# Two attention and GLU layers on one core: half of the values' products of the second layer as three f16 rounds, the GLU remainder on GpSimd

## The chip, the cores and the metric

The kernel runs on one core of one Trainium2 chip. The metric is device time in microseconds (us) of one execution; lower is better. The kernel before takes 2244.29 us, the median of 3 runs (2242.11 to 2247.71). The engines are written as the profile writes them: PE is TensorE (PEld its weight loads), DVE is VectorE, ACT is ScalarE, POOL is GpSimd, SP is SyncE, which issues most DMAs.

## The reference

x is 1 x 2048 x 448 in f32. There are 16 heads of 28, with one key head and one value head that all query heads share. F is 1792.

```python
def _A_ref(x, wq, wk, wv, wo):
    q = (x @ wq).reshape(B, S, H, Dh).transpose(0, 2, 1, 3)
    k, v = x @ wk, x @ wv
    p = softmax(einsum("bhqd,bkd->bhqk", q, k) * Dh ** -0.5)
    o = einsum("bhqk,bkd->bhqd", p, v)
    return o.transpose(0, 2, 1, 3).reshape(B, S, H * Dh) @ wo

def _B_ref(x, w_gate, w_up, w_down):
    return (sigmoid(x @ w_gate) * (x @ w_up)) @ w_down

x = x + _A_ref(layernorm(x), ...)      # layer 1
x = x + _B_ref(layernorm(x), ...)
x = x + _A_ref(layernorm(x), ...)      # layer 2, same weights
x = x + _B_ref(layernorm(x), ...)
```

## The kernel before

**Tiling.** The 2048 positions are cut into 16 *units* of 128 queries. In each layer a unit `u` runs through 16 *steps* `kt`, one for each 128 keys; so a layer has 256 steps. The 16 heads lie in 4 groups `g` of 4 heads, so that one group's queries make a moving operand of 4 x 128 = 512 columns. Two consecutive steps, an even and an odd one, are called a *pair* below.

**One step.** `scores` multiplies 128 keys with the queries of a group into the PSUM tile `s` (128 x 512, f16 operands), and ACT takes the exponent of `s` into the f32 SBUF tile `P`; four times in a step. `pv` multiplies `P` with the values `VV` (f32, 32 columns: 28 of the values and a column of ones for the softmax's sum). Its four matmuls, one for each group, occupy four different strips of 32 columns of the array (`tile_position=(0, 32 * g)`) and run at the same time; they add into one PSUM tile `pv` over the 16 steps. Each f32 matmul stands in the trace as two records. `Maxima.step` computes scores of a later unit against all keys (tiles `mx`, four matmuls at a time in four strips of 32 rows) and DVE reduces each `mx` tile to a row maximum; the maxima enter the scores of that later unit through an extra row. So in layer 2 DVE makes four reductions of 128 x 512 in each step up to unit 14.

**Order.** Every engine runs its instructions in the order in which the program writes them. The order is set by strings in `PATHS`: S is a `scores`, P a `pv` of the oldest waiting step, M a `Maxima.step`, X a tick of the side work, F a slice of filler. In layer 2, units 4 to 13 use D0 (even units) and D1 (odd units), units 14 and 15 E0 and E1. The first string of each serves even steps, the second odd steps. Both P of a pair stand in the even step and take the two steps of the pair before it. Filler is all other TensorE work, metered by `Filler.slice`: the GLU's gate and up products (`gp`, `up`), the down products (`dn`) and the output projection (`wo`). Work of other engines that follows a filler product is put off by `defer(fn, lag)` and written out at a later slice (`flush`).

**GLU.** Per block of 256 positions, 7 times: ACT makes `th` = tanh of the gate product, DVE makes (th + 1) x up in `th` (L756), ACT rounds it to f16 as `h[:, 0]` (L759), and DVE makes the remainder `h[:, 1]` (L760). `dn` multiplies both with the f16 halves of `w_down`.

**Side work of a unit** comes once in 16 steps, through ticks: the softmax sums go out and come back by DMA (`sums`, `rc`, `lb`), GpSimd multiplies (`lb`, L671), ACT and DVE split into two f16 parts (`oT`, L677 and L678), then the `wo` products, then on DVE the residual (L693) and the layer norm's statistics (L292, L293), six small GpSimd instructions for the reciprocal root (`rs`, L308 to L313), on DVE `xn` and `hl` (L331, L323), on GpSimd the remainder of `hl` (L324, L325).

**PSUM.** All tiles but `pv` share one ring of 7 banks (tag "f"). A matmul that opens a new tile waits until the tile that had the bank seven tiles earlier has been read by DVE or ACT.

Of the kernel before, what the change touches and what calls it, by code (L numbers as in the profile page):

```python
# [19 lines left out]
def interleaved_layers_kernel(ctx: ExitStack, tc: tile.TileContext, x, wq, wk, wv, wo, wg, wu, wd, out, layers=2):  # L20
# [147 lines left out]
    def prep_b():  # L168
# [75 lines left out]
        nc.vector.tensor_scalar(gsc, pwb[:, 1:2], 2.0 ** -26, None, op0=OP.mult)  # L244
# [40 lines left out]
    def ln_stats(*xts, fast=False):  # L285

        n = len(xts)
        mv = wk1.tile([128, 4, 2], F32, name="mv", bufs=4)
        r = wk1.tile([128, 4, 4], F32, name="rs", bufs=4)
        for i, xt in enumerate(xts):  # L290
            st = wk1.tile([128, 6], F32, name="st", bufs=3)
            nc.vector.bn_stats(st, xt)  # L292
            nc.vector.bn_aggr(mv[:, i], st)  # L293
        return (rstd_v if fast else rstd)(mv, r, n)
# [11 lines left out]
    def rstd(mv, r, n, bias=False):  # L306
# [5 lines left out]
        nc.gpsimd.tensor_scalar(z, z, -1024.0, 3072.0, op0=OP.mult, op1=OP.add)  # L312
# [52 lines left out]
    KK, VV, QH = {}, {}, {}  # L365

    def layer_tiles(l):
# [215 lines left out]
    def scores(l, u, kt, g, P):  # L583
# [4 lines left out]
        p = wk1.tile([128, 512], F32, tag="P", name="P", bufs=14)  # L588
        nc.scalar.activation(p, s, AF.Exp, scale=esc)  # L589
        P.append(p)  # L590

    def pv(l, u, kt, P):
# [3 lines left out]
        for g in range(4):  # L596
            nc.tensor.matmul(v[32 * g:32 * g + 32], VV[l][:, kt], P[g], start=kt == 0, stop=kt == KT - 1,  # L597
                             tile_position=(0, 32 * g))
# [25 lines left out]
    class Block:  # L624
# [8 lines left out]
        def tile(self, u):  # L633
# [53 lines left out]
            def wo_products():  # L687
# [4 lines left out]
                def f():  # L692
                    nc.vector.scalar_tensor_tensor(self.x1[:, t], p, osc, v["xr"], op0=OP.mult, op1=OP.add)  # L693
                    v["ls"] = ln_stats(self.x1[:, t])[0]
# [39 lines left out]
        def bulk(self):  # L734
# [3 lines left out]
            def glu(f):  # L738
# [15 lines left out]
                def ev():  # L754
# [3 lines left out]
                    def parts():  # L758
                        nc.scalar.activation(h[:, 0], t, AF.Copy, scale=2.0 ** -17)  # L759
                        defer(lambda: nc.vector.scalar_tensor_tensor(h[:, 1], t, 2.0 ** -17, h[:, 0], op0=OP.mult,  # L760
                                                                     op1=OP.subtract), 3)
# [272 lines left out]
    for b in range(1, NB):  # L1034
# [15 lines left out]
        "D0": ("FXFFSSSSPPM", "FSFSFXSFFMS"),  # L1050
        "D1": ("SFFXSFSSPPM", "SFSFFFXSFSFM"),
# [130 lines left out]
```

## Time and profile before

| | |
|---|---|
| median of 3 runs | 2244.29 us (2242.11 to 2247.71) |
| profiled execution, span from first to last instruction | 2242.6 us |
| mean granted TensorE clock | 0.996 |
| PE busy, share of the span | 98% |
| DVE busy | 73% |
| ACT busy | 69% |
| POOL busy | 15% |
| units 4 to 15 of layer 2 | about 1410 to 2157 us |
| one unit there | 62 to 64 us; unit 15: 52 us |

In rows of groups the two numbers after the bar are the busy time in us and the mean of one instruction in ns, then the engine's idle time before them with what ended it. In rows of a timeline the first number is the start in us, the second the duration; a merged row lasts from the first start to the last end, and brackets hold the idle time before it. Consecutive matmuls overlap in the trace, so the time a matmul costs is read from the start of the next one.

### The profile page before, as it was taken

What the parts mean: (1) busy time and instruction counts of PE and PEld (TensorE: products, weight loads), DVE (VectorE), ACT (ScalarE), POOL (GpSimd) and SP (SyncE); (2) the same over time, 40 slices, a digit from 0 to 9 for tenths busy, and PEclk for the clock granted to TensorE, in tenths of its full rate; (3) what the DMA queues carried; (4) which work ended last, traced back from release to release, by engine and by line L of the source; (5) the groups of instructions that cost most, each with busy time, mean ns of one, the idle gap of its engine ahead of it and who ended that gap; (6) DMA issues with size and microseconds to landing.
All of it is one profiled execution on the core that took longest, in us unless ns stands there. A gap on an engine that the chain in (4) does not pass through costs nothing.

```text
span 2242.6 us, 41405 instructions
## 1 busy us (share of the span) xinstructions
PE 2197.5 (98%) x15922; PEld 1032.1 (46%) x15922; DVE 1633.7 (73%) x2902; ACT 1556.5 (69%) x2603; POOL 328.6 (15%) x567
## 2 busy tenths in 40 slices
PE   7899999999999999999999999999999999999999
PEld 3322344444444444454564334445454545445457
DVE  7888887778778777777796557777777777777222
ACT  5698887777667677676514997777676767777741
POOL 4123764001110100101011010000000000000010
PEclk9999999999999999999999999999999999999999
DMA  5232662324323132422441123232231313132333
GB/s 174 70 98 87 209 211 83 105 62 118 98 67 102 58 109 61 127 78 69 135 136 40 31 56 113 52 107 80 86 101 58 107 50 104 56 107 78 97 105 118
DMA packets 203622, 213.28 MB, mean 95 GB/s; under 512 B 135376, under 2 KB 164240, under 8 KB 203424
## 3 DMA queue, kind: packets, MB, share of 16 engines
q1 hardware_dynamic: 198880, 195.88, 29.6%
q0 software_dynamic: 4544, 14.77, 1.7%
q8 instruction: 124, 2.03, 0.4%
q14 instruction: 74, 0.61, 0.1%
HBM read 175.37 MB, written 23.59 MB: 89 GB/s over the span
## 4 chain that ended last, share of the span: by engine, by line
PE 86%; DVE 4%; DMA 2%; ACT 2%; issue 1%; SPq 1%; POOL 0%; ACTq 0%; POOLq 0%; DVEq 0%
PE pv L597 20%; PE s L586 20%; PE dn L786 11%; PE gp L354 11%; PE up L354 11%; PE mx L551 7%; PE wo L697 3%; DVE mp L556 3%; PE qp L354 2%; ACT P L589 1%; DMA rc<-sums 1%; DMA sums<-rc 0%; DMA rgu<-in_B_w_gate_dram 0%; DMA lb<-sums 0%; PE hot L918 0%
## 5 line engine op out<-in xcount | busy, mean ns | idle before, releaser
L589 ACT ACTIVATE P<-s,esc 128x512 f32<-128x512 f32 x2048 | 1295.7, 692 | 455.8 <-PE s L586 444.6
L556 DVE TENSOR_REDUCE mp<-mx 128x1 f32<-128x512 f32 x2048 | 1269.6, 683 | 387.1 <-PE mx L551 382.7
L586 PE MATMUL s<-QS,KK 96*128 96x512 f16 x2048 | 687.0, 382 | 13.3 <-DVE mp L556 9.0
L354 PEld LDWEIGHTS <-wgu 128*128 128x128 f16 x4928 | 470.6, 97 | 174.6 <-issue 30.1
L597 PE MATMUL pv<-P,VV 128*32 128x512 f32 x4096 | 510.3, 602 | 0.0
L354 PE MATMUL gp<-XT,wgu 128*128 128x256 f16 x2464 | 350.3, 272 | 0.8 <-DVE mp L556 0.8
L354 PE MATMUL up<-XT,wgu 128*128 128x256 f16 x2464 | 347.7, 272 | 0.0
L786 PE MATMUL dn<-WD,h 128*128 128x448 f16 x1344 | 299.9, 352 | 0.0
L586 PEld LDWEIGHTS <-KK 96*128 96x128 f16 x2048 | 190.7, 97 | 232.6 <-issue 142.2
L597 PEld LDWEIGHTS pv<-P,VV 128*32 128x32 f32 x4096 | 98.7, 108 | 240.1 <-issue 238.9
L551 PE MATMUL mx<-KK,QH 32*128 32x512 f16 x1792 | 186.8, 384 | 5.3 <-DVE mp L556 1.9
L786 PEld LDWEIGHTS <-h 128*128 128x128 f16 x1344 | 127.1, 97 | 127.6 <-issue 11.2
L551 PEld LDWEIGHTS <-QH 32*128 32x128 f16 x1792 | 46.5, 91 | 247.8 <-issue 245.4
L671 POOL TENSOR_TENSOR lb<-pvs,lb 128x512 f32<-128x512 f32 x32 | 41.2, 1287 | 622.3 <-DMA lb<-sums 548.7
L759 ACT ACTIVATE h<-th 128x512 f16<-128x512 f32 x112 | 70.4, 628 | 67.4 <-DVE th L756 67.3
L308 POOL TENSOR_SCALAR rs<-mv 128x1 f32<-128x1 f32 (+1 forms) x50 | 12.2, 244 | 678.0 <-DVE mv L293 676.0
L354 PE MATMUL qp<-XT,WQ 128*128 128x512 f16 x352 | 109.5, 389 | 1.0 <-DVE mp L556 0.7
L756 DVE SCALAR_TENSOR_TENSOR th<-th,up 128x512 f32<-128x512 f32 x112 | 76.2, 680 | 42.2 <-PE up L354 36.7
L748 ACT ACTIVATE th<-gp,gsc 128x512 f32<-128x512 f32 x112 | 76.8, 686 | 32.3 <-PE gp L354 32.2
L760 DVE SCALAR_TENSOR_TENSOR h<-th,h 128x512 f16<-128x512 f32 x112 | 77.0, 688 | 29.6 <-ACT h L759 29.6
L697 PE MATMUL wo<-WO,oT 128*128 128x448 f16 x384 | 88.8, 352 | 0.9 <-ACT oT L677 0.5
L354 PEld LDWEIGHTS <-WQ 128*128 128x128 f16 x352 | 33.6, 99 | 49.7 <-issue 23.1
(158 smaller groups left out, 908.2 us busy)
## 6 DMA issues: line engine op xcount, KB each, us to landing
wgu<-wgu_d SPq DMA_DIRECT2D x224, 512.0 KB
QS<-qd SPq DMA_DIRECT2D x384, 32.0 KB
lb<-sums SPq DMA_DIRECT2D x128, 64.0 KB
xr<-in_A_x_dram SPq DMA_DIRECT2D x32, 224.0 KB
qd<-qst POOLq DMA_DIRECT2D x28, 256.0 KB, 2.6
wgu_d<-sgu POOLq DMA_DIRECT2D x14, 512.0 KB, 4.0
x2d<-x SPq DMA_DIRECT2D x16, 224.0 KB
xr<-x2d SPq DMA_DIRECT2D x16, 224.0 KB
```

Source lines behind the costliest of these rows:

```text
L354: nc.tensor.matmul(ps, a, b, start=n == 0, stop=n == 10)
L551: nc.tensor.matmul(ps[h][:, i * w:(i + 1) * w], qh[32 * h:32 * h + 32, g], KK[l][32 * h:32 * h + 32, 1, ka:kz], start=True, stop=True, til ...
L556: nc.vector.tensor_reduce(o, ps[h].rearrange("p (g k) -> p g k", g=n), axis=AX.X, op=OP.max)
L586: nc.tensor.matmul(s, KK[l][0:96, 0, kt * 128:(kt + 1) * 128], QS[l, u][:, g].rearrange("p h n -> p (h n)"), start=True, stop=True)
L589: nc.scalar.activation(p, s, AF.Exp, scale=esc)
L597: nc.tensor.matmul(v[32 * g:32 * g + 32], VV[l][:, kt], P[g], start=kt == 0, stop=kt == KT - 1, tile_position=(0, 32 * g))
L697: nc.tensor.matmul(p, v["oT"][:, a, h * 128:(h + 1) * 128], WO[:, c, h], start=n == 0, stop=n == 11)
L748: defer(lambda: nc.scalar.activation(th, gp.rearrange("p j n -> p (j n)"), AF.Tanh, scale=gsc))
L756: nc.vector.scalar_tensor_tensor(t, th, 1.0, up.rearrange("p j n -> p (j n)"), op0=OP.add, op1=OP.mult)
L759: nc.scalar.activation(h[:, 0], t, AF.Copy, scale=2.0 ** -17)
L760: defer(lambda: nc.vector.scalar_tensor_tensor(h[:, 1], t, 2.0 ** -17, h[:, 0], op0=OP.mult, op1=OP.subtract), 3)
L786: nc.tensor.matmul(p, hs[f // 2][:, a, o:o + 128], WD[:, f, c], start=n == 0, stop=n == 3 * FC - 1)
```

## The change

In layer 2, for even steps of units 4 to 15 (12 units x 8 steps = 96 steps), `P` and the values are each split into two f16 parts, high and remainder, and `pv` makes three rounds of four f16 matmuls (high x high, high of P x remainder of V, remainder of P x high of V) where it made four f32 matmuls. The high part of P is cast by DVE for groups 0 and 1 and by ACT for groups 2 and 3; the remainder is a GpSimd subtraction for all four. The parts lie in tiles `PH` of the pool `big`, three pairs of parts to a tile. The values' parts `VH` are made by GpSimd when layer 2's values are made. The ring of `P` shrinks from 14 to 13 tiles. The GLU remainder `h[:, 1]` moves from DVE to GpSimd in both layers, and is now a plain subtraction: the power-of-two factor 2^-17 has moved into the layer norm's factor and the scales. The strings D0 and D1 are written anew.

```diff
+            if l in VH:
+                nc.gpsimd.tensor_copy(VH[l][:, kt, 0], VV[l][:, kt])
+                nc.gpsimd.tensor_tensor(VH[l][:, kt, 1], VV[l][:, kt], VH[l][:, kt, 0], op=OP.subtract)
...
-        p = wk1.tile([128, 512], F32, tag="P", name="P", bufs=14)
+        p = wk1.tile([128, 512], F32, tag="P", name="P", bufs=13)
         nc.scalar.activation(p, s, AF.Exp, scale=esc)
-        P.append(p)
+        if not halved(l, u, kt):
+            P.append(p)
+            return
+        if not hold or hold[1] == 3:
+            hold[:] = [big.tile([128, 7, 512], F16, tag="big", name="PH"), 0]
+        t, n = hold
+        hold[1] += 1
+        hi, lo = t[:, 2 * n], t[:, 2 * n + 1]
+        P.append((hi, lo))
+        how = HI[g]
+
+        def part():
+            if how == "a":
+                nc.scalar.copy(hi, p)
+            else:
+                (nc.vector if how == "d" else nc.gpsimd).tensor_copy(hi, p)
+            nc.gpsimd.tensor_tensor(lo, p, hi, op=OP.subtract)
+        defer(part, HLAG)
+
+    hold = []
+    HI, HLAG = "ddaa", 2
+
+    def halved(l, u, k):
+        return l and u > 3 and k % 2 == 0
...
-        for g in range(4):
-            nc.tensor.matmul(v[32 * g:32 * g + 32], VV[l][:, kt], P[g], start=kt == 0, stop=kt == KT - 1,
-                             tile_position=(0, 32 * g))
+        if halved(l, u, kt):
+            flush(True)
+            for n, (a, c) in enumerate(((0, 0), (1, 0), (0, 1))):
+                for g in range(4):
+                    nc.tensor.matmul(v[32 * g:32 * g + 32], VH[l][:, kt, a], P[g][c],
+                                     start=kt == 0 and n == 0, stop=kt == KT - 1 and n == 2,
+                                     tile_position=(0, 32 * g))
+        else:
+            for g in range(4):
+                nc.tensor.matmul(v[32 * g:32 * g + 32], VV[l][:, kt], P[g], start=kt == 0, stop=kt == KT - 1,
+                                 tile_position=(0, 32 * g))
...
                     def parts():
-                        nc.scalar.activation(h[:, 0], t, AF.Copy, scale=2.0 ** -17)
-                        defer(lambda: nc.vector.scalar_tensor_tensor(h[:, 1], t, 2.0 ** -17, h[:, 0], op0=OP.mult,
-                                                                     op1=OP.subtract), 3)
+                        nc.scalar.copy(h[:, 0], t)
+                        nc.gpsimd.tensor_tensor(h[:, 1], t, h[:, 0], op=OP.subtract)
                     defer(parts, 3)
...
-        "D0": ("FXFFSSSSPPM", "FSFSFXSFFMS"),
-        "D1": ("SFFXSFSSPPM", "SFSFFFXSFSFM"),
+        "D0": ("FSFSXFSSPPM", "FSFFSXSFFMS"),
+        "D1": ("FSFSXFSSPPM", "FSFSFXSFSFM"),
```

Three places in the order of the instructions follow. The first is TensorE's order at the two P of a pair in layer 2. Before, with the last `scores` ahead of it and the first maxima behind it (`VV` values, `QH` queries for the maxima):

```order
L586 LDWEIGHTS KK
L586 MATMUL s<-QS,KK 128x512
L597 MATMUL pv<-P,VV 32x512 x8
L551 LDWEIGHTS QH
L551 MATMUL mx<-KK,QH 128x512
```

After, the last two of the twelve f16 matmuls and what follows them:

```order
L629 LDWEIGHTS VH
L629 MATMUL pv<-PH,VH 32x512
L629 LDWEIGHTS VH
L629 MATMUL pv<-PH,VH 32x512
L634 MATMUL pv<-P,VV 32x512 x4
L557 LDWEIGHTS QH
L557 MATMUL mx<-KK,QH 128x512
```

Eight f32 matmuls for the two steps have become twelve f16 matmuls, each with a weight load of its own, and four f32 matmuls; nothing else stands between the scores and the maxima.

The second place is DVE's order in unit 8, where `wo` has been added up (L693, now L730). Before:

```order
L756 SCALAR_TENSOR_TENSOR th<-th,up 128x512
L556 TENSOR_REDUCE mp<-mx 128x1 x4
L678 TENSOR_TENSOR oT<-lb,oT 128x512
L556 TENSOR_REDUCE mp<-mx 128x1 x4
L760 SCALAR_TENSOR_TENSOR h<-th,h 128x512
L556 TENSOR_REDUCE mp<-mx 128x1 x4
L693 SCALAR_TENSOR_TENSOR x_21100<-wo,osc,xr 128x448
L292 BN_STATS st<-x_21100 128x6
L293 BN_AGGR mv<-st 128x2
L556 TENSOR_REDUCE mp<-mx 128x1 x8
```

After:

```order
L793 SCALAR_TENSOR_TENSOR th<-th,up 128x512
L562 TENSOR_REDUCE mp<-mx 128x1 x4
L611 CAST PH<-P 128x512
L715 TENSOR_TENSOR oT<-lb,oT 128x512
L611 CAST PH<-P 128x512
L562 TENSOR_REDUCE mp<-mx 128x1 x8
L611 CAST PH<-P 128x512
L730 SCALAR_TENSOR_TENSOR x_21560<-wo,osc,xr 128x448
L293 BN_STATS st<-x_21560 128x6
L294 BN_AGGR mv<-st 128x2
L611 CAST PH<-P 128x512
L562 TENSOR_REDUCE mp<-mx 128x1 x8
```

Two casts of 128 x 512 stand ahead of the reductions that follow each pair's `pv`, mixed with what stood there before, and the remainder of `h` is gone.

The third place is GpSimd's order in one unit of layer 2, from the product `lb` to the first `rs` instructions. Before, nothing but the side work of a unit stands there:

```order
L671 TENSOR_TENSOR lb<-pvs,lb 128x512
L308 TENSOR_SCALAR rs<-mv 128x1
L309 TENSOR_TENSOR rs<-rs,mhalf 128x1
L310 TENSOR_TENSOR rs<-rs 128x1
L311 TENSOR_TENSOR rs<-rs 128x1
```

After:

```order
L708 TENSOR_TENSOR lb<-pvs,lb 128x512
L797 TENSOR_TENSOR h<-th,h 128x512
L612 TENSOR_TENSOR PH<-P,PH 128x512 x5
L309 TENSOR_SCALAR rs<-mv 128x1
L310 TENSOR_TENSOR rs<-rs,mhalf 128x1
L311 TENSOR_TENSOR rs<-rs 128x1
```

The remainders of P and of the GLU now stand around the side work, and those behind the first `rs` instruction wait behind it.

More of the change, by code (lines that the diff above doesn't have):

```diff
@@ L243, in prep_b @@
         yield from scales(mxb[:, 1:4], 3, pwb[:, 1:4], swb[:, 1:4])
-        nc.vector.tensor_scalar(gsc, pwb[:, 1:2], 2.0 ** -26, None, op0=OP.mult)
+        nc.vector.tensor_scalar(gsc, pwb[:, 1:2], 2.0 ** -16, None, op0=OP.mult)
+        nc.vector.tensor_scalar(swb[:, 2:3], swb[:, 2:3], 2.0 ** -7, None, op0=OP.mult)
         nc.vector.tensor_scalar(dsc, pwb[:, 2:3], pwb[:, 3:4], 2.0 ** -23, op0=OP.mult, op1=OP.mult)
@@ L282, in paced, with ln_stats @@
             prepd[0] += 1
-    def ln_stats(*xts, fast=False):
+    def ln_stats(*xts, fast=False, k=1024.0):
         n = len(xts)
@@ L293, in ln_stats @@
             nc.vector.bn_aggr(mv[:, i], st)
-        return (rstd_v if fast else rstd)(mv, r, n)
+        return rstd_v(mv, r, n) if fast else rstd(mv, r, n, k=k)
     def rstd_v(mv, r, n):
@@ L304, in rstd_v, with rstd @@
         return [(mv[:, 0, 0:1], w)]
-    def rstd(mv, r, n, bias=False):
+    def rstd(mv, r, n, bias=False, k=1024.0):
         v, y, z, w = (r[:, k, :n] for k in range(4))
@@ L311, in rstd @@
         nc.gpsimd.tensor_tensor(z, z, v, op=OP.mult)
-        nc.gpsimd.tensor_scalar(z, z, -1024.0, 3072.0, op0=OP.mult, op1=OP.add)
+        nc.gpsimd.tensor_scalar(z, z, -k, 3 * k, op0=OP.mult, op1=OP.add)
         nc.gpsimd.tensor_tensor(w, y, z, op=OP.mult)
@@ L364, in interleaved_layers_kernel @@
         nc.vector.memset(t[:, 0, 28:29], 32768.0)
-    KK, VV, QH = {}, {}, {}
+    KK, VV, VH, QH = {}, {}, {}, {}
     def layer_tiles(l):
@@ L371, in layer_tiles @@
         nc.vector.memset(VV[l][:, :, 28:29], 1.0)
+        if l:
+            VH[l] = lay.tile([128, KT, 2, 32], F16, tag="VH", name="VH", bufs=1)
     def kv(l, XT, t, kt):
@@ L693, in f @@
                     nc.vector.scalar_tensor_tensor(self.x1[:, t], p, osc, v["xr"], op0=OP.mult, op1=OP.add)
-                    v["ls"] = ln_stats(self.x1[:, t])[0]
+                    v["ls"] = ln_stats(self.x1[:, t], k=1.0)[0]
                 for h in range(4):
@@ L900, in load_x0 @@
         else:
-            xr0[i] = wk1.tile([128, D], F32, tag="P", name="xr0", bufs=14)
+            xr0[i] = wk1.tile([128, D], F32, tag="P", name="xr0", bufs=13)
         eng.dma_start(xr0[i], x[0, i * 128:(i + 1) * 128])
```

## The prediction

> **What bounds the kernel now.** I read the page's first part and its chain, then the busy times of stretches: one of layer 1, and the units of layer 2 that the change touches, one by one with their sum.
>
> ```profile
> span 2242.6 us, 41405 instructions
> PE 2197.5 (98%) x15922; PEld 1032.1 (46%) x15922; DVE 1633.7 (73%) x2902; ACT 1556.5 (69%) x2603; POOL 328.6 (15%) x567
> PE 86%; DVE 4%; DMA 2%; ACT 2%; issue 1%; SPq 1%; POOL 0%; ACTq 0%; POOLq 0%; DVEq 0%
> ```
>
> ```profile
> 700.00:900.00 200.00, 200.00 (x1494) 95.47 (x1492) 153.78 (x270) 144.41 (x237) 15.99 (x42) 1.00 0.27 78
> ...
> 1600.00:1663.00 63.00, 62.00 (x483) 31.60 (x482) 48.73 (x83) 46.58 (x75) 4.03 (x9) 1.00 0.35 108
> 1663.00:1727.00 64.00, 64.00 (x452) 28.89 (x448) 47.47 (x81) 44.57 (x71) 4.01 (x9) 1.00 0.20 58
> ...
> 2105.00:2157.00 52.00, 52.00 (x393) 28.32 (x392) 8.78 (x15) 40.66 (x70) 4.03 (x9) 1.00 0.38 119
> sum 747.00, PE 745.35 PEld 360.31 DVE 527.44 ACT 540.64 POOL 48.18; mean PE 62.11 PEld 30.03 DVE 43.95 ACT 45.05 POOL 4.01
> ```
>
> The windows' columns are length, then busy us of PE, PEld, DVE, ACT and POOL, clock, DMA. The sum covers units 4 to 15 of layer 2: PE is busy 745 of 747 us at full clock, DVE 71%, ACT 72%, POOL 6%. TensorE sets the time there. In layer 1 (the row from 700) PE is full too, so DVE's freed GLU time is worth nothing there.
>
> A busy PE is not yet a PE that could not be faster, so I read what it spends from starts:
>
> ```profile
> 1502.10 0.60 PE L586 MATMUL s<-QS,KK 96*128 96x512 f16 x2
> 1502.63 0.16 PEld L597 LDWEIGHTS pv<-P,VV 128*32 128x32 f32 x8 [0.42 <-issue]
> 1502.63 1.92 PE L597 MATMUL pv<-P,VV 128*32 128x512 f32 x16
> 1503.08 0.13 PEld L597 LDWEIGHTS pv<-P,VV 128*32 128x32 f32 x4 [0.30 <-issue]
> 1503.51 0.13 PEld L597 LDWEIGHTS pv<-P,VV 128*32 128x32 f32 x4 [0.30 <-issue]
> 1504.48 0.39 PE L551 MATMUL mx<-KK,QH 32*128 32x512 f16 x4
> 1504.81 0.39 PE L586 MATMUL s<-QS,KK 96*128 96x512 f16 x1
> ...
> 1609.10 0.93 PE L354 MATMUL up<-XT,wgu 128*128 128x256 f16 x7
> 1609.86 0.38 PE L586 MATMUL s<-QS,KK 96*128 96x512 f16 x1
> ```
>
> The pv of a pair starts at 1502.63 and the next work at 1504.48: 1.85 us for 16 records, which are four rounds of four strips. The loads that come with a new round start at 1503.08 and 1503.51, so a round is 0.43 us; 4 x 0.43 = 1.72, and some 0.13 is the change of form at its end. One f32 step is two rounds, 0.86 us. In f16, 7 x 256 columns take 0.76 us (1609.10 to 1609.86), that is 0.217 us for 512.
>
> **The change part by part.** *TensorE.* No f16 matmul in four column strips is in the trace. The floor is that a round costs one f16 matmul, as the f32 round costs two: 3 x 0.217 = 0.65 us, a saving of 0.21. The ceiling is the `mx` group, four f16 matmuls in row strips including its change of form: 1504.48 to 1504.81, 0.33 us; 3 x 0.33 = 0.99, a loss of 0.13. I take the floor, because the f32 rows are of the same strips: the next round's four loads take 0.13 us and fit inside a round of 0.22, and there is no change of form between rounds. 96 steps x 0.21 = **20.2 us** saved; by the ceiling 12.5 lost. A rule speaks against the floor: the Trainium skill, TensorE: Matmul & The Clock Gate, Part 3, says that a weight load overlaps a running matmul only when their row groups differ, and here all strips use the same rows. By it each round would also pay for its loads, near the ceiling. The f32 rows do not agree with it: loads are under way at 1503.08, and the rounds stay 0.43 apart.
>
> *VectorE.* Added are 192 casts (two in each of 96 steps), removed is the GLU remainder.
>
> ```profile
> L760 DVE SCALAR_TENSOR_TENSOR h<-th,h 128x512 f16<-128x512 f32 x41 | 27.7, 675 | 13.6 <-ACT h L759 13.6
> ...
> L323 DVE CAST hl<-xn 128x448 f16<-128x448 f32 x32 | 13.0, 408 | 1.1
> L137 POOL TENSOR_TENSOR sgu<-rgu,sgu 128x512 f16<-128x512 f32 x10 | 11.8, 1176 | 0.8
> L143 POOL TENSOR_TENSOR sgu<-rgu,sgu 128x512 f16<-128x512 f32 x9 | 10.4, 1160 | 0.7
> L677 ACT CAST oT<-lb 128x512 f16<-128x512 f32 x32 | 19.8, 619 | 6.0 <-POOL lb L671 6.0
> ...
> 254.52 0.84 DVE L323 CAST hl<-xn 128x448 f16<-128x448 f32 x1
> 254.74 2.06 POOL L136 TENSOR_SCALAR rgu<-rgu,swb 128x512 f32<-128x512 f32 x1
> ```
>
> A cast of 448 columns takes 0.41 us, 0.47 scaled to 512. The one at 254.52 ran beside GpSimd work and took 0.84, or 0.96 scaled; the GpSimd operation beside it took 2.06. So a cast costs 0.47 to 0.96, 90 to 184 us in all. 41 GLU remainders fall in these units (the first row is of them alone), 28 us less. DVE's load rises from 527 to between 589 and 683 of some 727 us: it does not become the bound as an average. Whether PE is held up depends on the free time just ahead of a pair's first maxima, where the casts stand:
>
> ```profile
> 1608.09 2.48 DVE L556 TENSOR_REDUCE mp<-mx 128x1 f32<-128x512 f32 x4 [1.66 <-PE mx L551]
> ...
> 1630.27 0.68 DVE L678 TENSOR_TENSOR oT<-lb,oT 128x512 f16<-128x512 f32 x1
> 1632.01 2.48 DVE L556 TENSOR_REDUCE mp<-mx 128x1 f32<-128x512 f32 x4 [1.06 <-PE mx L551]
> ...
> 1638.27 0.68 DVE L693 SCALAR_TENSOR_TENSOR x<-wo,osc,xr 128x448 f32<-128x448 f32 x1
> 1638.98 0.63 DVE L292 BATCH_NORM_STATS2 st<-x 128x6 f32<-128x448 f32 x1
> 1639.64 0.18 DVE L293 BATCH_NORM_AGGREGATE mv<-st 128x2 f32<-128x6 f32 x1
> 1640.16 2.48 DVE L556 TENSOR_REDUCE mp<-mx 128x1 f32<-128x512 f32 x4 [0.34 <-PE mx L551]
> ```
>
> In a plain pair DVE waits 1.66 us for the maxima, and two casts (0.94 alone, 1.43 with one of them beside GpSimd) are hidden by it; if that cover were gone, they would cost PE what exceeds the slack of the PSUM ring. That slack is small: the first of the four reductions from 1608.09 ends about 1608.78, and the `up` tile opened at 1609.10 above, which has the same bank by the program's allocation, takes it 0.32 us later. Behind `oT` the room is 1.06: short by up to 0.37, hardly more than the slack. Behind the residual and its statistics it is 0.34: short by 0.60 to 1.09, so the reductions are late and TensorE stands 0.3 to 0.8 us. The pair in which a unit's row maxima end has other small DVE work, and I give it half of that; even units have somewhat more room. Over a unit I take 0.6 us, over the ten units 4 to 13 **6 us**.
>
> *ScalarE.* 192 casts at 0.62 are 119 us: 541 becomes 660 of 727, 91%. Its exponents wait for TensorE now:
>
> ```profile
> ACT P L589 <- PE s L586: 191.1, 262, 1.8
> POOL lb L671 <- DMA lb<-sums: 319.3, 12, 30.9
> POOL rs L308 <- DVE mv L293: 225.1, 12, 22.2
> ```
>
> These waits, of units 4 to 15, are 191 us, more than the casts need. The new `flush` ahead of pv writes put-off work out at once, so ACT's rounding of `h` may stand behind DVE's `th` for up to one DVE instruction, 41 x 0.68 = 28 us at most; the same waits hide that. Only unit 15 is dense, 52 us long and with ACT busy for 41 of them; there 16 casts (10 us) leave about 1 us, and unit 14 has an ACT cast of `oT` that now may wait for a `lb` that GpSimd delivers late. I take **1.5 us** for the two units.
>
> *GpSimd.* The remainders are priced by the rows L137 and L143 above (f16 out of f32, 128 x 512), the side work by these:
>
> ```profile
> L671 POOL TENSOR_TENSOR lb<-pvs,lb 128x512 f32<-128x512 f32 x32 | 41.2, 1287 | 622.3 <-DMA lb<-sums 548.7 <-ACT P L589 73.6
> L309 POOL TENSOR_TENSOR rs<-rs,mhalf 128x1 f32<-128x1 f32 x47 | 27.5, 585 | 3.9
> L310 POOL TENSOR_TENSOR rs<-rs 128x1 f32<-128x1 f32 x47 | 9.1, 195 | 3.7
> ```
>
> 384 remainders and some 41 of the GLU at 1.16 are 493 us: 48 becomes 541 of 727, 74%. A pair lasts 7.9 us now (63 us for 8), 7.7 after; four remainders are 4.64, with one of the GLU 5.8, with `lb` besides 7.1. It fits. Since GpSimd serves in order, the `lb` product no longer waits 30.9 us idle ahead of its DMA; it comes later than the DMA, and the remainders behind it are not held. The `rs` instructions are the delicate place: their six take about 1.6 us (0.59 and five of some 0.2) and wait for DVE's statistics, with three remainders of P queued behind them, which the third round of the next pair's pv reads. 4.64 + 1.6 + some 0.5 of waiting = 6.7, against some 7 us from a pair's first cast to that round. I take nothing for it and keep it for a rival. The GLU remainder is off every path: `dn` reads it many products later. The 32 small instructions for `VH` are done in layer 1's end, before unit 4 needs them.
>
> *Strings, rings.* D0 and D1 hold as many S, P and M as before, and filler is metered by the count of F; with the scores less bunched the casts start earlier. With 13 tiles a P comes round after some three steps, and pv reads it, or GpSimd does, within two and a half. The `PH` ring holds 15 pairs of parts, 3.75 halved steps, against a pv one halved step later. I cost both at nothing; if a P came late, ACT would stand, and the 191 us cover it.
>
> Sum: 2242.6 - 20.2 + 6 + 1.5 = 2229.9 for a profiled execution. The median of the runs shown is 1.7 us above the span, so 2231.6; I say **2231 us**, 0.6% faster.
>
> **The rivals.** *Nothing stands in the way.* The room behind `oT` and the statistics suffices because the pv before is shorter and the order is looser; then 2242.6 - 20.2 + 1.7 = 2224. For it: TensorE has no other wait in these units. Against it: the 0.34 us row.
>
> *GpSimd late.* The remainders behind `rs`, `lb` and the GLU remainder come 0.3 to 0.5 us after the third round asks for them, in some three pairs of each unit: about 1.2 us a unit, 12 in all, on top of my 7.5. Then 2231.6 + 12 = 2243.6, no change. For it: 6.7 of 7 us. Against it: only the third round needs them, and the average load is 74%.
>
> *VectorE and GpSimd hinder each other (slower).* If every cast takes 0.96, two are 1.92: plain pairs are short by 0.26 and still pass, but behind the statistics 1.58 is missing, behind `oT` and behind `xn` 0.86 each, in the maxima's last pair some 1.4. Less 0.32 of slack each, that is about 3.5 us a unit, 35 in ten: 2242.6 + 1.7 - 20.2 + 35 = 2259. It decides from 2 us a unit (20.2 / 10). For it: the row at 254.52. Against it: one row; the second cast of a pair can start right behind the first, ahead of the remainder that waits for the first.
>
> *Loads not hidden (slower).* Rounds cost 0.33: 12.5 lost where I have 20.2 gained; 2242.6 + 1.7 + 12.5 + 7.5 = 2264. This is what the rule on row groups would give here. Against it: the f32 rounds.
>
> **How the numbers follow.** Chances: my forecast 0.55 (2225 to 2238 of its own), nothing in the way 0.13, GpSimd late 0.17, mutual hindrance 0.10, loads not hidden 0.05. About 0.3% (6.7 us) is what a measurement of this kernel can tell from no change, so faster means below 2237.5. Faster: 0.50 of the 0.55, 0.13, and 0.01 of the third, 0.64. Same: 0.05 and 0.13, 0.18. Slower: 0.03 of the third, 0.10 and 0.05, 0.18. The range reaches from 2222, the full gain and a little more, to 2248, which holds the case of no change and leaves the two slower ones out.
>
> **What would show it.** In the changed profile a pair's pv should take about 1.64 us from its first start to the maxima (1.85 less 0.21), with rounds 0.22 apart; 1.98 would show the loads. Units 4 to 13 should last about 62 us where they lasted 63, and DVE's row of idle time ahead of `mx` should fall from 1.66 to about 0.5 in plain pairs and vanish behind the statistics, with PE idle there, ended by DVE. The casts' mean tells the hindrance: 0.5 for mine, 0.9 or more for the rival. PE waiting for GpSimd by more than 1 us a unit makes the third case. ACT above 95% busy before unit 15 would prove my sum wrong, and so would a changed time of layer 1 by more than 3 us.

## The result, and the profile after

The change takes **2234.09 us** (median of 5 runs, 2231.74 to 2234.86); the kernel before, on the same chip, 2245.64 (5 runs, 2242.11 to 2247.72; the three runs shown ahead of the prediction are among them). The ratio is **0.9945, 95% interval 0.9934 to 0.9956**: faster, by 0.55%. The forecast was 2231 us, 0.6% faster, with a range of 2222 to 2248.

The profiled execution of the change, first part of the page:

```profile
span 2232.5 us, 43041 instructions
PE 2181.6 (98%) x16306; PEld 1037.2 (46%) x16306; DVE 1661.5 (74%) x2983; ACT 1652.0 (74%) x2795; POOL 910.0 (41%) x1095
```

To see where the time went I use one ruler for all kernels below: ACT's copy of the finished `pv` tile, which ends every unit. The view of the tile `pvs` from 1400 us on gives the first such copy (end of unit 3) and the last (end of unit 15). Before, then the change:

```profile
L601 ACT COPY pvs<-pv x13: 586/586/587, 1410.0 to 2156.8; 128x512 f32<-128x512 f32 x13
```

```profile
L638 ACT COPY pvs<-pv x13: 586/597/620, 1413.3 to 2146.7; 128x512 f32<-128x512 f32 x13
```

Units 4 to 15 of layer 2 took 746.8 us and take 733.4: **13.4 us less**. All that comes ahead of them took 1410.0 and takes 1413.3; what follows takes 85.8 us in both (2242.6 - 2156.8, 2232.5 - 2146.7). The 13.4 us are not spread evenly: by the same copies unit 6, an even one, went from 64.15 to 62.34 us, unit 11, an odd one, from 61.73 to 61.63.

What `pv` itself saved is more. Summed over the 96 pairs, from a pair's first `pv` matmul to the start of the next work, it took 177.0 us before and takes 155.2: 21.7 us less. Of these 8.3 are lost again elsewhere.

The groups of the added work (of the whole execution; those of P and `PH` lie in units 4 to 15 alone), and the busy time in units 4 to 15 (columns as in the prediction's windows):

```profile
L612 POOL TENSOR_TENSOR PH<-P,PH 128x512 f16<-128x512 f32 x384 | 443.0, 1178 | 132.2 <-DVE PH L611 130.8 <-PE mx L557 0.7 <-PE pv L634 0.7
L797 POOL TENSOR_TENSOR h<-th,h 128x512 f16<-128x512 f32 x112 | 130.9, 1168 | 454.4 <-ACT h L796 454.4
L609 ACT CAST PH<-P 128x512 f16<-128x512 f32 x192 | 110.2, 633 | 0.0
L611 DVE CAST PH<-P 128x512 f16<-128x512 f32 x192 | 106.1, 578 | 31.8 <-ACT P L595 31.7
L629 PE MATMUL pv<-PH,VH 128*32 128x512 f16 x1152 | 80.4, 383 | 0.2 <-POOL PH L612 0.2
```

```profile
1413.30:2146.70 733.40, 728.24 (x5865) 365.04 (x5862) 598.38 (x1050) 636.79 (x1063) 539.29 (x533) 1.00 0.28 85
```

ScalarE's casts and GpSimd's remainders cost what was forecast (0.633 and 1.178 us), VectorE's casts 0.578 in the mean. In these units VectorE is 82% busy, ScalarE 87%, GpSimd 74%. The waits of TensorE that end at GpSimd come to 0.2 us in all.

Now one pair, in odd unit 7, which has `oT`'s subtraction in it: TensorE, then VectorE from this pair to the next, then GpSimd (time lines).

```profile
1628.24 0.83 PE L629 MATMUL pv<-PH,VH 128*32 128x512 f16 x12
1628.90 1.03 PE L634 MATMUL pv<-P,VV 128*32 128x512 f32 x8
1629.87 0.39 PE L557 MATMUL mx<-KK,QH 32*128 32x512 f16 x4
...
1631.19 0.38 PE L592 MATMUL s<-QS,KK 96*128 96x512 f16 x1
1632.26 0.60 PE L355 MATMUL up<-XT,wgu 128*128 128x256 f16 x4 [0.70 <-DVE mp L562]
...
1637.19 0.83 PE L629 MATMUL pv<-PH,VH 128*32 128x512 f16 x12
```

```profile
1628.67 1.04 DVE L611 CAST PH<-P 128x512 f16<-128x512 f32 x1
1629.63 0.68 DVE L715 TENSOR_TENSOR oT<-lb,oT 128x512 f16<-128x512 f32 x1
1630.23 1.38 DVE L611 CAST PH<-P 128x512 f16<-128x512 f32 x1
1631.53 2.47 DVE L562 TENSOR_REDUCE mp<-mx 128x1 f32<-128x512 f32 x4
...
1637.35 0.42 DVE L611 CAST PH<-P 128x512 f16<-128x512 f32 x1
1637.68 0.68 DVE L730 SCALAR_TENSOR_TENSOR x<-wo,osc,xr 128x448 f32<-128x448 f32 x1
...
1639.16 0.40 DVE L611 CAST PH<-P 128x512 f16<-128x512 f32 x1
1639.47 2.48 DVE L562 TENSOR_REDUCE mp<-mx 128x1 f32<-128x512 f32 x4
```

```profile
1628.26 1.17 POOL L797 TENSOR_TENSOR h<-th,h 128x512 f16<-128x512 f32 x1 [0.65 <-ACT h L796]
1629.79 1.54 POOL L612 TENSOR_TENSOR PH<-P,PH 128x512 f16<-128x512 f32 x1 [0.36 <-DVE PH L611]
...
1637.85 1.16 POOL L612 TENSOR_TENSOR PH<-P,PH 128x512 f16<-128x512 f32 x1 [2.71 <-DVE PH L611]
```

The three f16 rounds take 0.66 us (1628.24 to 1628.90), the pair 1.63 to the maxima at 1629.87 (1.85 before). Then TensorE goes on until 1631.19 and opens the next `up` only at 1632.26, behind a reduction: 1.07 us from start to start, where such a step takes 0.22 elsewhere, so TensorE stands for 0.85. The reductions began at 1631.53, 1.66 us after the first `mx` matmul: two casts of 1.04 and 1.38 us, with `oT`'s subtraction between them, stood in front of them. Behind the statistics, in the next pair, the casts take 0.42 and 0.40.

Casts and GpSimd's work explain each other. The cast at 1628.67 starts while GpSimd's remainder of `h` runs (it ends at 1629.43) and ends at 1629.71, 0.28 us later. The cast at 1630.23 starts beside the remainder that ends at 1631.33 and ends at 1631.61, again 0.28 us later. In units 4 to 15, 57 of the 192 casts start while GpSimd works, and 53 of them end 0.28 to 0.30 us after GpSimd's instruction; they take 1.0 us in the median, up to 1.40. Three of the other four start in its last 0.08 us, and one beside the first small `rs` instruction; these take 0.41 to 0.43. The 135 casts that start while GpSimd is idle take 0.39 to 0.43, also the 67 during which a GpSimd instruction begins. This looks like a lock: VectorE's cast waits for GpSimd's instruction to end and then does most of its work. The reductions (545 start beside GpSimd) and the product `th` (25) take 0.68 beside GpSimd as alone.

The Trainium skill, SBUF — State Buffer, "Who interferes with whom", states it: VectorE and GpSimd share a pair of SBUF ports, and the pair is an exclusive lock; a cast can take both ports, and then whoever issues first holds the pair for its whole instruction; a subtraction of two SBUF operands contends with what GpSimd reads, and a reduction never contends. The rows agree, and bring the 0.28 us.

In each of the odd units 5 to 13 the pair with `oT` looks like this one: it lasts 8.95 us (1628.24 to 1637.19), and a cast of 1.04 and one of about 1.38 us lie around the subtraction. In the even units the cast behind `oT` takes 1.40 us too, yet no gap of this size is found there.

### The profile page after: what moved, and what is told of

It reads as the page before. It is cut to its first block, busy times and chain, and to the rows that moved or that the text cites. A ratio compares the mean times of both kernels' runs of the same rounds, so it can differ in the third digit from the quotient of the medians.

```text
span 2232.5 us, 43041 instructions
## 1 busy us (share of the span) xinstructions
PE 2181.6 (98%) x16306; PEld 1037.2 (46%) x16306; DVE 1661.5 (74%) x2983; ACT 1652.0 (74%) x2795; POOL 910.0 (41%) x1095
## 4 chain that ended last, share of the span: by engine, by line
PE 86%; DVE 5%; ACT 2%; DMA 1%; issue 1%; SPq 1%; POOL 1%; DVEq 0%; ACTq 0%; POOLq 0%
PE s L592 19%; PE pv L634 16%; PE dn L822 11%; PE gp L355 11%; PE up L355 11%; PE mx L557 7%; DVE mp L562 3%; PE wo L734 3%; PE pv L629 3%; PE qp L355 2%; ACT P L595 2%; DVE PH L611 1%; DMA sums<-rc 0%; SPq L453 0%; POOL PH L612 0%
## 5 line engine op out<-in xcount | busy, mean ns | idle before, releaser
L592 PE MATMUL s<-QS,KK 96*128 96x512 f16 x2048 | 694.9, 382 | 13.4 <-DVE mp L562 8.6
L612 POOL TENSOR_TENSOR PH<-P,PH 128x512 f16<-128x512 f32 x384 | 443.0, 1178 | 132.2 <-DVE PH L611 130.8
L634 PE MATMUL pv<-P,VV 128*32 128x512 f32 x3328 | 425.5, 601 | 0.0
L355 PE MATMUL gp<-XT,wgu 128*128 128x256 f16 x2464 | 357.1, 272 | 0.5 <-ACT P L595 0.2
L355 PE MATMUL up<-XT,wgu 128*128 128x256 f16 x2464 | 354.0, 273 | 3.5 <-DVE mp L562 3.5
L797 POOL TENSOR_TENSOR h<-th,h 128x512 f16<-128x512 f32 x112 | 130.9, 1168 | 454.4 <-ACT h L796 454.4
L634 PEld LDWEIGHTS pv<-P,VV 128*32 128x32 f32 x3328 | 81.9, 109 | 162.6 <-issue 141.8
L611 DVE CAST PH<-P 128x512 f16<-128x512 f32 x192 | 106.1, 578 | 31.8 <-ACT P L595 31.7
L309 POOL TENSOR_SCALAR rs<-mv 128x1 f32<-128x1 f32 (+1 forms) x50 | 13.4, 268 | 266.4 <-DVE mv L294 264.1
L796 ACT CAST h<-th 128x512 f16<-128x512 f32 x112 | 69.2, 618 | 61.9 <-DVE th L793 61.0
L609 ACT CAST PH<-P 128x512 f16<-128x512 f32 x192 | 110.2, 633 | 0.0
```

The source lines that it names most:

```text
L355: nc.tensor.matmul(ps, a, b, start=n == 0, stop=n == 10)
L592: nc.tensor.matmul(s, KK[l][0:96, 0, kt * 128:(kt + 1) * 128], QS[l, u][:, g].rearrange("p h n -> p (h n)"), start=True, stop=True)
L609: nc.scalar.copy(hi, p)
L611: (nc.vector if how == "d" else nc.gpsimd).tensor_copy(hi, p)
L612: nc.gpsimd.tensor_tensor(lo, p, hi, op=OP.subtract)
L797: nc.gpsimd.tensor_tensor(h[:, 1], t, h[:, 0], op=OP.subtract)
```

## The experiments

The first theory, from the profile: **the lock at `oT`**. The saving is there, and a good part of it is lost again because GpSimd's new work lengthens VectorE's casts where `oT` leaves no room. The rival, my forecast on record: casts that take no longer than 0.47, late behind the statistics, by VectorE's load.

In each, "units" means units 4 to 15 by the ruler, in the profiled execution. How well units of layer 2 repeat, the first run below says.

**The change once more**

> The change itself, unaltered, beside the run above on the same chip. By the pattern so far (units of the second layer repeat within 0.02 us, the first four units of the first layer differ by up to 5 us between executions) units 4 to 15 take 733.4 us again, within 0.3, wherever the first layer ends (1105.8 to 1110.8 us so far), and the whole 2232 to 2235. If units 4 to 15 differ by over 1 us, the accounts by units are no measure.

The ruler's row:

```profile
L638 ACT COPY pvs<-pv x13: 585/592/620, 1412.8 to 2146.2; 128x512 f32<-128x512 f32 x13
```

Units 733.4 again, every one of them within 0.03 us; the whole 2233.84 us, ratio 0.9955 (0.9941 to 0.9969). The kernel before is less exact there: with the same code in its second layer it took 746.8 us, and 745.3 in the run with the shorter ring below. What is saved against it is uncertain by these 1.5 us.

**GpSimd's remainders of P left out**

```diff
-            nc.gpsimd.tensor_tensor(lo, p, hi, op=OP.subtract)
...
-                    nc.tensor.matmul(..., VH[l][:, kt, a], P[g][c],
+                    nc.tensor.matmul(..., VH[l][:, kt, a], P[g][0],
```

> The change without GpSimd's remainders of P: the 384 subtractions are left out, and the third round of each halved step multiplies the rounded part again, so that the same number of products run but the output lacks the remainder's share. Theory A, a lock: in the change each VectorE cast that starts while GpSimd works ends 0.28 us after GpSimd's instruction ends (55 of 192 casts, 1.01 us in the median and up to 1.40, against 0.42 alone). With GpSimd at some 16 per cent busy, nearly all casts take 0.42 us, their mean falls from 0.58 to below 0.47; TensorE's stalls of 1.2 us in each odd unit fall to 0.5 or less, and units 4 to 15 take 726 to 729 us instead of 733.4. Theory B, it is the sum of work on VectorE that counts, not the hindrance: the casts keep their places, and units 4 to 15 take 732 us or more.

The ruler, then TensorE's `pv` of the pair with `oT` in unit 7 and of the next, and VectorE's time line at `oT`:

```profile
L637 ACT COPY pvs<-pv x13: 586/595/619, 1413.8 to 2140.5; 128x512 f32<-128x512 f32 x13
```

```profile
1627.56 0.83 PE L628 MATMUL pv<-PH,VH 128*32 128x512 f16 x12
...
1635.52 0.83 PE L628 MATMUL pv<-PH,VH 128*32 128x512 f16 x12
```

```profile
1627.98 0.98 DVE L611 CAST PH<-P 128x512 f16<-128x512 f32 x1
1628.88 0.68 DVE L714 TENSOR_TENSOR oT<-lb,oT 128x512 f16<-128x512 f32 x1
1629.48 0.41 DVE L611 CAST PH<-P 128x512 f16<-128x512 f32 x1
1629.82 2.47 DVE L562 TENSOR_REDUCE mp<-mx 128x1 f32<-128x512 f32 x4
```

Units **726.7**, the whole 2227.08 (0.9917, 0.9903 to 0.9930). That is 20.1 us less than before, with all casts still on VectorE and ScalarE. At `oT` the first cast still meets the remainder of `h`, the second takes 0.41, and the pair lasts 7.96 us (1627.56 to 1635.52) instead of 8.95; odd units take 60.62. The mean of VectorE's casts is 0.483, a little above the expected 0.47. So the 6.7 us between this and the change are the price of GpSimd's 384 remainders. Pair by pair they lie at `oT` in the five odd units (0.99 each, 5.0 together), in units 14 and 15 (1.3), and the little that is left mostly in the even units.

The casts themselves, ScalarE's and VectorE's, and the new order cost less: `pv` is 22.2 us shorter here than before (154.8 against 177.0), and the units 20.1 (18.6 against the 745.3), so 2 to 3.6 us go elsewhere. No run takes these apart.

**The GLU remainder back on VectorE**

```diff
-                        nc.gpsimd.tensor_tensor(h[:, 1], t, h[:, 0], op=OP.subtract)
+                        defer(lambda: nc.vector.tensor_tensor(h[:, 1], t, h[:, 0], op=OP.subtract), 3)
```

> The change with its GLU remainder back on VectorE (a subtraction there, put off by three steps as before). Theory A, collision: the 1.2 us by which TensorE stands in each odd unit from 7 to 15, in the pair of the rounding of oT, come from GpSimd's GLU remainder (1.17 us) beside a cast that takes 1.04 instead of 0.42; without it the stall falls to 0.6 or less, units 4 to 15 take 728 to 731 us instead of 733.4, and the whole is 2229 to 2232 us. Theory B, the sum of VectorE's work is what counts: 41 more subtractions of 0.68 us there (28 us, from 81 to 85 per cent busy) make more reductions late; units 4 to 15 take 735 us or more, the whole 2235 to 2238.

The ruler, then the time lines of VectorE and of GpSimd from the pair with `oT` in unit 7 on:

```profile
L638 ACT COPY pvs<-pv x13: 585/592/612, 1413.5 to 2160.7; 128x512 f32<-128x512 f32 x13
```

```profile
1633.25 1.56 DVE L715 TENSOR_TENSOR oT<-lb,oT 128x512 f16<-128x512 f32 x1 [0.23 <-ACT oT L714]
1634.73 0.68 DVE L797 TENSOR_TENSOR h<-th,h 128x512 f16<-128x512 f32 x1
...
1650.54 1.55 DVE L797 TENSOR_TENSOR h<-th,h 128x512 f16<-128x512 f32 x1
```

```profile
1633.10 1.16 POOL L612 TENSOR_TENSOR PH<-P,PH 128x512 f16<-128x512 f32 x1 [2.03 <-DVE PH L611]
```

Units **747.2**, the whole 2248.57 (1.0012, 1.0004 to 1.0021): no gain is left. My expectation by the lock (2229 to 2232) was wrong, and the rival's (2235 to 2238) not far enough. I had looked only at the cast that the remainder of `h` holds up. With that remainder gone from GpSimd, the remainder of P starts ahead of `oT`'s subtraction, by 0.15 us (1633.10), where it started 0.16 behind it in the change; now the subtraction meets it: 1.56 us instead of 0.68. The subtractions of `h` on VectorE meet GpSimd too: the 14 that start beside it take 0.92 to 1.66 us, 1.55 in the median, and end 0.55 us after GpSimd's instruction. Whether this is the lock or VectorE's load, the next run tells.

**The same, and GpSimd's remainders of P left out**

> The change with the GLU remainder back on VectorE, and without GpSimd's 384 remainders of P (the third round multiplies the rounded part again, so the output lacks the remainder's share). With the remainders of P, that place of the GLU remainder made units 4 to 15 13.8 us longer than the change (747.2 against 733.4). Theory A, the lock: there the subtractions of oT and h took 1.55 us on VectorE beside GpSimd, 0.68 alone; without GpSimd's work all take 0.68, and units 4 to 15 take 726 to 731 us (726.7 with the GLU remainder on GpSimd and the remainders of P left out). Theory B, the sum of VectorE's work: the 28 us of subtractions cost the same 13 us here; units 4 to 15 take 737 to 741 us.

The ruler, and two groups of VectorE from 1400 us on:

```profile
L637 ACT COPY pvs<-pv x13: 585/593/617, 1414.2 to 2144.6; 128x512 f32<-128x512 f32 x13
```

```profile
L611 DVE CAST PH<-P 128x512 f16<-128x512 f32 x192 | 78.0, 433 | 28.3 <-ACT P L595 28.0
L796 DVE TENSOR_TENSOR h<-th,h 128x512 f16<-128x512 f32 x47 | 32.3, 687 | 12.3 <-ACT h L795 12.2
```

Units 730.5, the whole 2231.82 (0.9933, 0.9917 to 0.9950). On a GpSimd without the remainders of P, the GLU remainder on VectorE costs 730.5 - 726.7 = 3.8 us; beside them 13.8. So 3.8 is VectorE's load, and the other 10 arise only where that work and GpSimd's remainders come together. The rows of 1.55 and 1.56 us above point to the lock for them; how much of the 10 each kind of wait costs is not shown.

**The GLU remainder on GpSimd alone**, in the kernel before:

```diff
-                        nc.scalar.activation(h[:, 0], t, AF.Copy, scale=2.0 ** -17)
-                        defer(lambda: nc.vector.scalar_tensor_tensor(h[:, 1], t, 2.0 ** -17, h[:, 0], op0=OP.mult,
-                                                                     op1=OP.subtract), 3)
+                        nc.scalar.copy(h[:, 0], t)
+                        nc.gpsimd.tensor_tensor(h[:, 1], t, h[:, 0], op=OP.subtract)
```

> One part of the change alone, put into the kernel before: the remainder of the GLU product goes from VectorE to GpSimd in both layers (with the scales that this needs); no value product is halved, and the strings and rings are those of before. The question is the 3 to 4 us by which the profiled change comes out of layer 1 later than the kernel before (1109.7 against 1105.8 us). Theory A: those microseconds are the GLU remainder's doing, since GpSimd prepares weights in the same stretch; then this kernel too leaves layer 1 some 3 us later, and the whole is 2 to 4 us slower than before (ratio 1.001 to 1.002). Theory B: they differ from one execution to the next; then layer 1 ends within 1.5 us of before, and the whole is 0 to 2 us faster (TensorE's stalls in units 4 to 15 of layer 2 are only 2.7 us before, so no more can be won).

Units 746.7 (1411.3 to 2158.0), the whole 2245.02, ratio 1.0004 (0.9995 to 1.0013): worth nothing by itself. Its first layer ends at 1107.9 us, between the two theories' marks. The whole is nearer to the second, though the small gain that it allowed isn't seen either.

**The shorter ring of P alone**, in the kernel before:

```diff
-        p = wk1.tile([128, 512], F32, tag="P", name="P", bufs=14)
+        p = wk1.tile([128, 512], F32, tag="P", name="P", bufs=13)
...
-            xr0[i] = wk1.tile([128, D], F32, tag="P", name="xr0", bufs=14)
+            xr0[i] = wk1.tile([128, D], F32, tag="P", name="xr0", bufs=13)
```

> The kernel before with one edit: the ring of P tiles has 13 tiles instead of 14. It tests what the change costs outside units 4 to 15 of the second layer: those are 13.4 us shorter in the change, the whole only 10 to 11.5 by the medians. Theory A: the shorter ring delays layer 1; then this kernel is 1.5 to 3 us slower than before (ratio 1.0007 to 1.0013), and its first layer ends later than 1107 us. Theory B: the ring is as free as I costed it, and the rest is chance of single executions; then the ratio is 1.000 within 0.0007.

The same view of its first layer, from the end of unit 0 to the end of unit 15:

```profile
L601 ACT COPY pvs<-pv x16: 574/586/604, 153.3 to 1110.2; 128x512 f32<-128x512 f32 x16
```

The whole 2245.56, ratio 0.9998 (0.9989 to 1.0007): nothing. Units 745.3 (1412.7 to 2158.0). Its profiled first layer ended at 1110.2 us, later than the change's 1109.7, and it still took 2243.7 us in all. The end of layer 1 differs between executions of the same instructions by more than the 3.9 us that I had seen between the two kernels: eight profiled executions here have the change's first layer, and it ended between 1106.7 and 1110.8 us. I found no part of the change to blame.

**The strings of the kernel before**, in the change:

```diff
-        "D0": ("FSFSXFSSPPM", "FSFFSXSFFMS"),
-        "D1": ("FSFSXFSSPPM", "FSFSFXSFSFM"),
+        "D0": ("FXFFSSSSPPM", "FSFSFXSFFMS"),
+        "D1": ("SFFXSFSSPPM", "SFSFFFXSFSFM"),
```

> The change with the strings D0 and D1 of the kernel before; only the order of scores, filler and products in units 4 to 13 differs. Theory A, the strings matter: they spread a pair's scores so that the exponents, and with them the casts that GpSimd's remainders wait for, come earlier; without that the third round of pv waits for GpSimd or the casts are late ahead of the maxima; units 4 to 15 take 738 to 745 us instead of 733.4, the whole 2239 to 2246. Theory B, they are worth nothing, as I costed them: units 4 to 15 take 732 to 735 us, the whole 2232 to 2236.

The ruler, and two groups from 1400 us on:

```profile
L638 ACT COPY pvs<-pv x13: 586/595/618, 1412.2 to 2150.1; 128x512 f32<-128x512 f32 x13
```

```profile
L611 DVE CAST PH<-P 128x512 f16<-128x512 f32 x192 | 112.9, 606 | 39.1 <-ACT P L595 38.4
L629 PE MATMUL pv<-PH,VH 128*32 128x512 f16 x1152 | 81.2, 382 | 1.1 <-POOL PH L612 1.1
```

Units 737.9, the whole 2238.62 (0.9966, 0.9953 to 0.9978). The strings are worth 4.5 us, a hair under what the first theory wanted and far from nothing. TensorE waits for GpSimd 1.1 us instead of 0.2, and 75 casts instead of 57 start beside GpSimd's work. That the order acts through these two is likely; no run takes it apart.

**Casts behind the statistics moved to ScalarE**

```diff
-        how = HI[g]
+        how = "a" if u % 2 and kt == 10 else HI[g]
```

> The change with one edit: in the odd units, the four casts of key step 10 (behind the residual and its statistics) are all ScalarE's; 12 casts move in all. Theory A, collision at oT: behind the statistics TensorE stands for some 0.15 us only, so no more than 1 us is gained, the whole is 2233 to 2235 us. Theory B, my forecast on record: the statistics cost 0.3 to 0.8 us in each of these units, so that 2 to 4 us are gained, the whole 2230 to 2232.

Units 735.6 (1412.9 to 2148.5), the whole 2236.10 (0.9961, 0.9948 to 0.9975): 2.2 us worse than the change, not better. The stall that I had put there isn't there to be won, and ScalarE's extra casts cost something of their own, half of it in unit 15 (51.59 us instead of 50.46).

**Casts at `oT` moved to ScalarE, all four**

```diff
-        how = HI[g]
+        how = "a" if u % 2 and kt == 8 else HI[g]
```

> The change with one edit: in the odd units, the four casts of key step 8 (those that stand around oT's remainder) are all ScalarE's instead of two VectorE's and two ScalarE's; 12 casts move in all. Theory A, collision at oT: the stall of 1.2 us in each odd unit from 7 to 15 goes, five units by 1.0 to 1.2 us are 5 to 6 us; units 4 to 15 take 728 us, the whole 2228 to 2230. Theory B, my forecast on record (the place is behind the statistics, key step 10): nothing is gained here, and ScalarE, which rounds oT and h in the same pair, has 1.3 us more to do there, so units 4 to 15 take 733 to 736 us, the whole 2234 to 2237.

VectorE, ScalarE and TensorE in the pair with `oT` of unit 7 (time line):

```profile
1628.48 0.39 PE L557 MATMUL mx<-KK,QH 32*128 32x512 f16 x4
1628.90 2.48 DVE L562 TENSOR_REDUCE mp<-mx 128x1 f32<-128x512 f32 x4 [0.28 <-PE mx L557]
...
1629.45 1.66 ACT L609 CAST PH<-P 128x512 f16<-128x512 f32 x3
1631.00 1.28 ACT L595 ACTIVATE P<-s,esc 128x512 f32<-128x512 f32 x2
...
1631.76 0.38 PE L592 MATMUL s<-QS,KK 96*128 96x512 f16 x1 [0.19 <-ACT P L595]
```

Units 733.5 (1412.0 to 2145.5), the whole 2232.11 (0.9946, 0.9933 to 0.9958): no gain, as the rival wanted, but not for its reason. The stall behind VectorE is gone: the reductions begin 0.42 us after `mx` (1628.48) instead of 1.66. In its place ScalarE, with three casts in a row behind one more, reads the score tiles late, and TensorE waits for it several times; odd units take 61.51 instead of 61.62. In unit 15 (51.17 instead of 50.46) the same edit costs 0.7.

**Three by ScalarE, one by VectorE**

```diff
-        how = HI[g]
+        how = "daaa"[g] if u % 2 and u < 14 and kt == 8 else HI[g]
```

> The change with one edit: in key step 8 of the odd units 5 to 13 three of the four casts are ScalarE's and one is VectorE's (two and two in the change; all four ScalarE's gave VectorE its room back, but then TensorE waited for ScalarE's exponents, by as much). Theory A, both engines fit with this split: VectorE is free for the maxima when they come, ScalarE has 0.57 us less than with four; the odd units fall from 61.6 to 60.5 or 60.9 us, five of them save 4 to 5.5 us; units 4 to 15 take 728 to 730, the whole 2228 to 2231. Theory B, ScalarE's room ends already with the third cast: the odd units stay at 61.4 or more, the whole at 2232 to 2235.

TensorE in the pair with `oT` of unit 9 (time line):

```profile
1752.63 0.73 PE L734 MATMUL wo<-WO,oT 128*128 128x448 f16 x3 [0.41 <-ACT P L595]
```

Units 731.1 (1410.2 to 2141.4), the whole 2230.74 (0.9927, 0.9914 to 0.9939); odd units 61.18, between the two theories. VectorE is on time, ScalarE still late by one cast of 0.57, and `wo` waits for a bank that ScalarE has to read.

**One by VectorE, two by ScalarE, one by GpSimd**

```diff
-        how = HI[g]
+        how = "daag"[g] if u % 2 and u < 14 and kt == 8 else HI[g]
```

> The change with one edit: in key step 8 of the odd units 5 to 13 one cast is VectorE's, two are ScalarE's and the last is GpSimd's (three by ScalarE brought these units from 61.6 to 61.2 us, TensorE waiting 0.55 us for a score tile that ScalarE had not read yet). GpSimd idles 2.7 us behind that step's remainders. Theory A: with ScalarE's two casts as in the change and VectorE's room as with three, neither holds TensorE; the odd units fall to 60.6 (what they take when GpSimd's remainders are left out) or 60.9 us, units 4 to 15 take 728 to 729.5 us, the whole 2228 to 2230. Theory B: the longer stretch of GpSimd's work catches other casts of VectorE, or its cast of 0.6 to 1.2 us makes the third round late; the odd units stay at 61.2 or more, the whole at 2231 or more.

The ruler, and VectorE and GpSimd in the pair with `oT` of unit 9 (time line):

```profile
L638 ACT COPY pvs<-pv x13: 585/592/620, 1411.4 to 2139.9; 128x512 f32<-128x512 f32 x13
```

```profile
1749.72 0.68 DVE L715 TENSOR_TENSOR oT<-lb,oT 128x512 f16<-128x512 f32 x1
1750.38 2.48 DVE L562 TENSOR_REDUCE mp<-mx 128x1 f32<-128x512 f32 x4
...
1753.60 0.60 POOL L611 CAST PH<-P 128x512 f16<-128x512 f32 x1
```

Units **728.5**, the whole **2227.69** (0.9923, 0.9909 to 0.9938): faster than both kernels, 6.2 us below the change run beside it (2233.84). Odd units take 60.65, as without any remainder of P; the two at 60.84 and 60.87 (7 and 13) were longer by as much in the change. Of each such pair the second cast leaves VectorE for ScalarE, and ScalarE gives one of its two to GpSimd, which had a hole of 2.71 us there; five stalls of 1 us went with them. Together with the run without remainders, where the cast stays and takes 0.41, this shows the place and the cause: 5 us are lost in the pair with `oT`, because the second cast waits there for GpSimd's remainder and keeps the reductions waiting.

## Why the prediction was right, and where not

- **TensorE, 96 x 0.21 = 20.2 us: right, a little low.** Rounds are 0.22 us apart, a pair takes 1.63 us (forecast 1.64), and over all 96 pairs `pv` is 21.7 us shorter. The loads of the twelve matmuls are hidden. The rule of the Trainium skill, TensorE: Matmul & The Clock Gate, Part 3 (a weight load overlaps a running matmul only when the row groups differ), which was weighed against the f32 rows, is not borne out by the f16 rows either: four strips of the same rows come 0.22 us apart, and not near the ceiling of 0.33. That part of the Trainium skill also lets a load go ahead into a background weight buffer; whether that is what happens here, no row tells.
- **VectorE's lateness, 6 us in units 4 to 13: right in size, wrong in place and kind.** These units went from 631.3 to 621.1 us, 10.2 less where the forecast saved 16.8 (80 steps x 0.21), so 6.6 lost; 5.4 of them are GpSimd's remainders, since without these the units take 615.7. The step that failed is "Behind `oT` the room is 1.06: short by up to 0.37, hardly more than the slack. Behind the residual and its statistics it is 0.34 [...] and TensorE stands 0.3 to 0.8 us." Measured: the five waits of TensorE that end at VectorE (3.5 us) all lie in the pair with `oT`. Against the run without remainders that pair is 0.99 us longer in odd units and the pair of the statistics 0.02, and moving the casts behind the statistics gains nothing. I took a cast beside GpSimd as one that runs slower, up to 0.96; it is one that waits, 0.42 or up to 1.40. Behind the statistics GpSimd was waiting for the casts and for `mv`, so both took 0.4; at `oT`, in odd units, the `h` remainder and the remainder of the first cast held up one each. That the size agreed is chance: a wrong price in a wrong place.
- **The row at 254.52**, from which I took the 0.96, is of another kind: there GpSimd's instruction began 0.22 us after the cast. In the change 67 casts met a GpSimd instruction in this way and took 0.39 to 0.43. Why that one took 0.84 stays open.
- **The rival "VectorE and GpSimd hinder each other"** had the mechanism, with 0.10 and 35 us. Its price failed on "If every cast takes 0.96": 53 of 192 wait, by very different amounts, and mostly those at `oT` in odd units cost TensorE anything. The test on record, a mean of 0.5 for mine and 0.9 for the rival, came out at 0.578 and could not tell, since it averages two kinds of casts.
- **The GLU remainder, "28 us less"** on VectorE and "off every path": I gave the move no price of its own. Alone it is worth 0, with the halved products 13.8 us, the whole gain. Of this, 10 us arise only beside GpSimd's remainders of P.
- **Strings at nothing: wrong.** They are worth 4.5 us, which this forecast took for granted.
- **Units 14 and 15, 1.5 us: about right.** They went from 115.6 to 112.3 us, 3.3 less where 3.4 were saved, as if nothing were lost. But without GpSimd's remainders they take 111.0, so the remainders cost 1.3 here. The late `lb` of the forecast is in the trace: ScalarE stands 0.68 us ahead of its cast of `oT` (2061.47 us) until GpSimd has made `lb`, and `scores` then wait for ScalarE twice, by 0.2 us.
- **GpSimd late: hardly.** The waits of TensorE that end at GpSimd come to 0.2 us in all; it is one, at the last `pv` matmul of the third round in unit 15.
- **The ends.** The sum asked for -12.7 us in units 4 to 15, and they gave -13.4: 21.7 saved and 8.3 lost where 20.2 and 7.5 were forecast, two errors that cancel. The profiled execution of the change began unit 4 3.3 us later, and its median lies 1.6 us above its span: 2242.6 + 3.3 - 13.4 + 1.6 = 2234.1, where 2231 was forecast. By the bounds on record ("a changed time of layer 1 by more than 3 us" would prove the sum wrong) this counted against me. That test was too narrow, since the change's own layer 1 ended 4.1 us apart in the eight executions told of above. The kernel before, unedited, has one profiled execution (1105.8), so whether the change delays layer 1 by a microsecond or two is not shown.

## What to carry to other kernels

Before giving GpSimd a stream of work, list VectorE's casts and two-operand SBUF subtractions that can start beside it, and price each at the rest of GpSimd's instruction plus its own tail, not at a slower rate; what counts is which of them stand ahead of something that TensorE waits for. Where one engine has no room in one pair, a few instructions shared out to the engine that is idle in that pair can win back what a wholesale move to a busier one doesn't. Two parts of a change can be worth nothing each and everything together, so undo them one at a time.

## What the runs showed of the hardware

- A VectorE cast that started beside a GpSimd instruction ended 0.28 to 0.30 us after it, in 53 of 57 cases of the change (three of the others started in its last 0.08 us, one beside a small `rs` instruction); a VectorE subtraction of two SBUF operands 0.55 us after it (10 of `oT`, 14 of `h`, with the GLU remainder on VectorE). GpSimd waits in turn: its subtraction that began 0.16 to 0.22 us behind `oT`'s took 1.47 to 1.54 us instead of 1.17, in five cases.
- A cast during which a GpSimd instruction began took 0.39 to 0.43 us, in 67 cases of the change.
- VectorE's reductions out of PSUM (545) and its product with one operand in PSUM (25) took 0.68 us beside GpSimd and alone.
- f16 rounds of four column strips came 0.22 us apart with their loads hidden, as the f32 rounds at 0.43.
- GpSimd's cast of 128 x 512 from f32 to f16 took 0.60 us, half of its subtraction (1.18).
- A unit of layer 2 repeated within 0.03 us between executions of the change, while the end of layer 1 moved by up to 5 us (1105.8 to 1110.8 over all kernels here); so effects of a microsecond could be read from one profile by units, though not from the whole time.
